# A planned attention-and-feed-forward program, replaced by one explicit list of operations

## The chip, the cores and the metric

The kernel runs on one core of one Trainium2 chip. The metric is the device time of one execution, in microseconds (us); lower is better. The core's engines run side by side and meet at semaphores: TensorE (PE in the profile, with its weight loads as PEld), VectorE (DVE), ScalarE (ACT), GpSimd (POOL) and SyncE (SP, which here only issues transfers). Each engine takes its own instructions strictly in the order in which they stand, so that an instruction that waits holds up everything behind it on that engine.

## The reference

Routed attention, and then a feed-forward layer on its output, in float32:

```python
q_assign = argmax(einsum('bhsd,hcd->bhsc', q_n, c_n))      # q_n, k_n, c_n: rows divided by their norms
k_assign = argmax(einsum('bhsd,hcd->bhsc', k_n, c_n))
mask = q_assign[:, :, :, None] == k_assign[:, :, None, :]
scores = where(mask, q @ k.T / sqrt(D), -1e9)
attn = softmax(scores)
x = (attn @ v).transpose(0, 2, 1, 3).reshape(B * S, H * D)
h = x @ w_in
out = (h * sigmoid(h)) @ w_out
```

There are B = 4 batches of H = 8 heads, S = 768 positions, D = 64, 16 clusters for each head; w_in is 512 x 2048 and w_out 2048 x 512. The output has 3072 rows of 512.

## The kernel before

**Jobs and codes.** A job holds the rows of q and k of one head of one batch (jobs 0 to 7 and two extra ones, x0 and x1, for the first batch; jobs 8 to 31 for the three others). `load` (lines 107 to 113) brings its rows in as float32, with two transfers on SP's queue. `hi` and `lo` (lines 116 to 133) split them into two halves of float16. `xpose` (line 141) is one DMA transpose, issued by SP, that turns both halves so that the 64 features lie on partitions: tile `ab<-hl`. In the first batch TensorE does this instead (`tr`, line 155, and `ev`). `logits_n` (line 180) multiplies the transposed rows with the centroids: 12 small matmuls into `psN`. `lsum`, `mx_n` and `ge_n` on VectorE turn the result into a one-hot cluster code. Up to job 15 TensorE turns the code round and SP moves it below the features (`cd_mm`, `cd_ev`); from job 16 on a DMA transpose (`c_xpose`, line 233) and a move issued by GpSimd (`c_move`, line 237) do so. A score matmul over features and code then gives a masked score in one pass.

**Score units.** There are 192 units. `qk_mm` (line 354) makes one with two matmuls of 384 columns, `exp` (line 359) takes the exponential on ScalarE. `pv` (line 371) multiplies six units of two heads with the values in 36 small matmuls, `norm` divides, and either TensorE (`xn_t`) or a DMA transpose issued by SP (`xn_d`, line 412) turns the result into a piece of `xt`. `load_v` (line 290) brings the values of one head in, and `cast_v` on GpSimd makes them float16.

**Feed-forward.** For each half batch (b, c) there are 16 hidden blocks: `unit_a` is four matmuls with w_in (line 421, tile `ph`), a tanh on ScalarE (line 441) and a gating product on VectorE (line 444, tile `gt`); below, one of them is called a hidden unit. Then come the output products with w_out, directly (`part_b`, line 480) or, for 9 pairs of blocks, by a scheme with seven products in place of eight (class `Pair`, line 562). `w_load` (lines 618 and 621) brings the weights in by 12 transfers on GpSimd's queue, numbers 0 to 7 for w_in and 8 to 11 for w_out; the last two wait for the exponentials of units 22 and 23, by a small copy of one of their elements (line 614).

**What sets the order.** Up to unit 26 the order is a list, `plan`, written out by hand. From there a planner in the kernel's own code runs through the rest: it keeps a clock for each engine with assumed lengths, a list of waiting pieces for each, and takes the piece that is ready and has the lowest rank. Due times for loads and splits stand in tables (`SPLIT`, `AHEAD`, `VALUES`, `CAST`); assumed transfer times stand in `lands`, which starts with a backlog of 13.2 us; `ROOM`, `CODES` and `TURN` are margins behind a transfer. PSUM banks 0 to 3 are handed out from a list of free ones. Values of heads 16 to 31 are loaded by GpSimd (`value_free`), those of 8 to 15 by SP.

**The end.** The last pair's last product is made in two halves of 128 columns (`product` with a part, line 562). ScalarE copies one (line 609) and VectorE the other (line 607), and each goes out by a transfer of its own (line 610).

## Time and profile before

| | |
|---|---|
| median of three runs | 302.59 us (302.19 to 305.77) |
| the profiled execution's own time | 302.92 us |
| its span, first to last instruction | 301.1 us |
| mean granted TensorE clock | 0.994 |
| PE busy | 289.7 us, 96% of the span |
| ACT, DVE, POOL busy | 223.2, 223.1, 73.2 us |
| DMA moved | 45.16 MB, mean 150 GB/s |

In the profile a span of 40 slices shows the busy share of each engine in tenths. A matmul's duration in a row (327 ns for 384 columns) is longer than its share of the engine's time, since the next one starts before it ends: in a dense stretch four of them take 0.65 us. A wait is listed by the line that waits, the line that released it, the total, how often, and the longest. A transfer's "us to landing" runs from its issue to the time when the data are there.

### The profile page before, as it was taken

To read this page: it belongs to the slowest core of one execution; us is meant where nothing else is said; L and a number is where in the kernel's file an instruction comes from. 1 tells how busy PE (TensorE), PEld (TensorE's weight loads), DVE (VectorE), ACT (ScalarE), POOL (GpSimd) and SP (SyncE) were. 2 spreads that over 40 slices of the span, in tenths; PEclk is the share of its full clock that TensorE was granted. 3 is DMA by queue.
4 is the path that set the end of the run, shared out by engine and by line. 5 is a ranking of instruction groups with operands and counts; after the bars stand their busy time and mean duration, and the time that the engine had idled before them with its cause. 6 is when DMAs were issued, how large, how long until landed. Compare 5 with 4: busy or idle time off the path is not lost.

```text
span 301.1 us, 8269 instructions
## 1 busy us (share of the span) xinstructions
PE 289.7 (96%) x3305; PEld 206.5 (69%) x3305; DVE 223.1 (74%) x467; ACT 223.2 (74%) x365; POOL 73.2 (24%) x133
## 2 busy tenths in 40 slices
PE   7889899999999999999997999999999999999995
PEld 3767756666666566678754778776777767767784
DVE  5999569587999989897764679879746375468753
ACT  5869879856997679987894897977769888455420
POOL 2884630010240037533601250522200000000000
PEclk9999999999999999999997999999999999999999
DMA  6697899996997999998699599594311003110114
GB/s 215 192 233 150 232 196 224 181 247 178 266 249 180 230 211 165 251 198 165 172 122 188 157 172 269 108 181 95 73 48 38 15 15 96 37 35 0 37 35 142
DMA packets 79574, 45.16 MB, mean 150 GB/s; under 512 B 58384, under 2 KB 75568, under 8 KB 79536
## 3 DMA queue, kind: packets, MB, share of 16 engines
q1 hardware_dynamic: 74304, 36.14, 53.3%
q0 software_dynamic: 4800, 8.13, 14.7%
q8 instruction: 26, 0.43, 0.6%
q10 hardware_dynamic: 432, 0.36, 0.4%
q14 instruction: 12, 0.10, 0.1%
HBM read 27.30 MB, written 6.29 MB: 112 GB/s over the span
## 4 chain that ended last, share of the span: by engine, by line
PE 85%; DMA 9%; DVE 2%; ACT 1%; SPq 1%; issue 0%; ACTq 0%
PE ph L421 26%; PE pS L354 18%; PE po L562 18%; PE pO L371 10%; PE po L480 7%; DMA ab<-hl 4%; PE psN L180 3%; DMA ab<-cd 2%; DMA raw<-in_k_dram 1%; DMA raw<-in_q_dram 1%; DVE hl L132 1%; ACT P L359 1%; SPq L111 1%; PE px L393 0%; PE pTk L155 0%
## 5 line engine op out<-in xcount | busy, mean ns | idle before, releaser
L359 ACT ACTIVATE P<-pS 128x768 f16<-128x768 f32 x192 | 155.9, 825 | 32.8 <-PE pS L354 32.2
L421 PE MATMUL ph<-xt,win_s 128*128 128x384 f16 x512 | 98.2, 327 | 0.2 <-DVE gt L444 0.2
L354 PE MATMUL pS<-ab 128*128 128x384 f16 x384 | 93.4, 328 | 1.6 <-DMA ab<-cd 0.8
L444 DVE SCALAR_TENSOR_TENSOR gt<-tn,ph 128x384 f16<-128x384 f32 x110 | 59.1, 549 | 30.5 <-ACT tn L441 29.9
L421 PEld LDWEIGHTS <-win_s 128*128 128x128 f16 x512 | 49.4, 98 | 31.0 <-issue 0.7
L441 ACT ACTIVATE tn<-ph 128x384 f32<-128x384 f32 x110 | 55.0, 509 | 8.3 <-PE ph L421 7.4
L354 PEld LDWEIGHTS <-ab 128*128 128x128 f16 x384 | 34.5, 98 | 18.6 <-issue 1.2
L371 PEld LDWEIGHTS <-P 128*128 128x128 f16 x1152 | 39.9, 97 | 6.0 <-DVE gt L444 1.2
L371 PE MATMUL pO<-vt,P 128*128 128x65 f16 x1152 | 41.4, 193 | 0.6 <-DVE gt L444 0.5
L562 PEld LDWEIGHTS <-gt 128*128 128x128 f16 x336 | 31.8, 98 | 6.5 <-DVE gt L544 0.4
L132 DVE SCALAR_TENSOR_TENSOR hl<-raw,hl 128x768 f16<-128x768 f32 (+3 forms) x35 | 33.0, 945 | 1.6 <-ACT hl L123 1.3
L295 POOL CAST vt<-vn 128x384 f16<-128x384 f32 x32 | 18.3, 585 | 48.6 <-DMA vn<-in_v_dram 48.6
L562 PE MATMUL po<-wout_s,gt 128*128 128x256 f16 x216 | 27.7, 273 | 0.0
L480 PE MATMUL po<-wout_s,gt 128*128 128x512 f16 x96 | 24.5, 379 | 0.0
L224 POOL TENSOR_SCALAR od<-od 128x96 f16<-128x96 f16 x16 | 9.3, 579 | 59.6 <-DVE od L217 59.5
L180 PEld LDWEIGHTS <-ab 128*128 128x128 f16 x458 | 17.1, 97 | 5.8 <-DMA ab<-hl 2.3
L180 PE MATMUL psN<-stk,ab 128*128 128x32 f16 (+1 forms) x458 | 18.4, 188 | 1.9 <-DMA ab<-hl 1.9
L192 DVE TENSOR_REDUCE L<-psN 128x192 f32<-128x384 f32 (+1 forms) x27 | 14.8, 549 | 6.2 <-PE psN L180 6.1
L562 PE MATMUL po<-tw,sg 128*128 128x256 f16 x144 | 19.0, 281 | 0.0
L383 DVE TENSOR_TENSOR xn<-pO,zr 128x384 f16<-128x384 f32 x32 | 17.8, 558 | 1.1
L562 PEld LDWEIGHTS <-sg 128*128 128x128 f16 x144 | 14.3, 100 | 3.2 <-issue 0.3
L467 ACT ACTIVATE tn<-ph 128x768 f32<-128x768 f32 x9 | 7.3, 811 | 11.4 <-PE ph L421 11.4
(101 smaller groups left out, 264.5 us busy)
## 6 DMA issues: line engine op xcount, KB each, us to landing
raw<-in_k_dram SPq DMA_DIRECT2D x31, 192.0 KB, 3.6
out_dram<-ot SPq DMA_DIRECT2D x23, 256.0 KB, 2.3
raw<-in_q_dram SPq DMA_DIRECT2D x24, 192.0 KB, 3.6
vn<-in_v_dram SPq DMA_DIRECT2D x16, 192.0 KB, 4.1
vn<-in_v_dram POOLq DMA_DIRECT2D x16, 192.0 KB, 4.5
win_s<-in_moe_w_in_dram POOLq DMA_DIRECT2D x8, 256.0 KB, 5.9
wout_s<-in_moe_w_out_dram POOLq DMA_DIRECT2D x4, 512.0 KB, 16.1
cp<-gt SPq DMA_DIRECT2D x4, 256.0 KB, 4.3
```

What stands on the lines that cost most here:

```text
L132: nc.vector.scalar_tensor_tensor(out=hl[:, s, 1, :], in0=raws[job.name][:, s, :], scalar=QS, in1=hl[:, s, 0, :], op0=ALU.mult, op1=ALU.sub ...
L180: nc.tensor.matmul(L[:, n % g, :, n // g], ab[:, i, :], stk[:, job.groups[i // 3][0], x : x + w], start=(x == 0), stop=(x + w == 2 * HC),)
L295: nc.gpsimd.tensor_copy(vt[:, :, 0:D], vns.pop(i))
L354: nc.tensor.matmul(pS[:, e, 0:HALF], abs_[kj.name][:, kn, :], rhs, start=True, stop=True)
L359: nc.scalar.activation(out=P, in_=pst.pop(u)[:, :, 0:HALF], func=AF.Exp, bias=0.0, scale=ESC)
L371: nc.tensor.matmul(o[:, (2 * t + h) * VW : (2 * t + h + 1) * VW], Ps[i + h, c, j // 2][:, j % 2, ts(t, 128)], vtb[(i + h) % 13][:, j, 0:VW ...
L383: nc.vector.tensor_tensor(out=xn, in0=ov[:, :, 0:D], in1=zr.unsqueeze(2).to_broadcast([128, 2 * NM, D]), op=ALU.mult)
L421: nc.tensor.matmul(ph[:, 0:HALF], win_s[:, r, ts(fb, 128)], xts[b, c][:, r, :], start=(r == 0), stop=(r == NR - 1))
L441: nc.scalar.activation(out=tn, in_=ph[:, 0:HALF], func=AF.Tanh, bias=0.0, scale=1.0)
L444: nc.vector.scalar_tensor_tensor(out=gt[:, fb, :], in0=tn, scalar=1.0, in1=ph[:, 0:HALF], op0=ALU.add, op1=ALU.mult)
L480: nc.tensor.matmul(po, gts[b, c][:, fc, ts(t, 128)], wout_s[:, fc, :], start=(fc == 0), stop=(fc == NFB - 1))
L562: nc.tensor.matmul(o, l[:, f, :], x[:, x0 : x0 + w], start=(f == 0 and k in begins), stop=(f == HK - 1), skip_group_check=True)
```

## The change

The planner, the hand-written plan for the first part and the list of free PSUM banks go (some 650 lines). In their place stands one string, `order`, of some 1,550 words for the whole program, and a table `words` that maps each word to a function. A word is an operation, its job, unit or block, an engine letter where there is a choice, and after @ the PSUM banks. Instructions are issued in the order of the words; each engine's own order follows from it. The computation is the same, and so are the numbers of matmuls of each kind but for one: the last product is no longer cut in two.

Some steps that one function did are now two words, so that the second can stand later: the move of the code (`cd_go`) behind its eviction, the stores of output blocks (`part_store`, `second`, `second_last`, `third_last`) behind the copies. Of the values of heads 16 to 31, twelve are now loaded by SP (S); GpSimd keeps six loads in all (P: heads 10, 15, 18, 27, 29, 30). In the first part the high halves of jobs 5 and 7 move from GpSimd to ScalarE and that of job 6 from GpSimd to VectorE.

```diff
-    def cd_mm(job):
+    def cd_mm(job, bk=None):
...
-        done(psN)
-        nc.sync.dma_start(abs_[job.name][64 : 64 + HC, 0 : 2 * m, :].rearrange("p n c -> p (n c)"), o)
+        cds[job.name] = o
+
+    def cd_go(job):
+        m = (job.n + 1) // 2
+        nc.sync.dma_start(abs_[job.name][64 : 64 + HC, 0 : 2 * m, :].rearrange("p n c -> p (n c)"), cds.pop(job.name))
...
-        def c21_last(self, part):
-            x = slice(part * HD // 2, part * HD // 2 + HD // 2)
-            if part:
-                nc.vector.tensor_copy(self.ot2[:, x], self.A[:, x])
-            else:
-                nc.scalar.activation(out=self.ot2[:, x], in_=self.A[:, x], func=AF.Copy, bias=0.0, scale=1.0)
-            (nc.sync if part else nc.scalar).dma_start(self.rows()[:, 0, x], self.ot2[:, x])
+        def c21_last(self):
+            nc.scalar.activation(out=self.ot2[:, 0:HD], in_=self.A[:, 0:HD], func=AF.Copy, bias=0.0, scale=1.0)
+
+        def third_last(self):
+            nc.scalar.dma_start(self.rows()[:, 0, :], self.ot2[:, 0:HD])
...
-        if i >= 2 * H:
-            add("POOL", t, 0.6, lambda: load_v(i, nc.gpsimd), lambda t: got_v(i, t))
-        else:
-            add("SP", t, 0.7, lambda: load_v(i), lambda t: got_v(i, t))
...
+        ab.0.0.0@2 ce.x1.A nm.6.0 s.24 cg.x1 ab.0.0.2@3 x.24 ld.10 xp.6.0@0 ab.0.0.1@1 xe.6.0.D ae.0.0.0
+        ae.0.0.1 s.25 t.0.0.0 ab.0.0.7@0 x.25 g.0.0.0 ae.0.0.7 ae.0.0.2 lo.8 ab.0.0.6@2 t.0.0.7 t.0.0.1 ae.0.0.6
+        s.26 g.0.0.7 t.0.0.6 tp.8 s.27 t.0.0.2 ab.0.0.4@0 g.0.0.6 x.26 ae.0.0.4 g.0.0.1 ab.0.0.5@2 g.0.0.2 x.27
+        ae.0.0.5 ab.0.0.3@1 t.0.0.4 s.28 ae.0.0.3 g.0.0.4 s.29 t.0.0.3 au.0.0.10@3 t.0.0.5 g.0.0.3 x.28
+        au.0.0.8@0 g.0.0.5 au.0.0.9@1 x.29 pv.0.1@2 t.0.0.8 t.0.0.9 hi.10.A g.0.0.9 s.31 s.30 nm.0.1 au.0.0.11@1
+        x.30 g.0.0.8 L.8.32@2 t.0.0.10 hi.11.D au.0.0.12@0 t.0.0.11 ls.8 x.31 s.32 g.0.0.11 au.0.0.13@2 g.0.0.10
...
+        "tp": lambda x, k: xpose(key_job(x[0])),
+        "L": lambda x, k: logits_n(key_job(x[0]), k and k[0], int(x[1]), range(int(x[2]), int(x[3])) if x[2:] else None),
+        "s": lambda x, k: qk_mm(int(x[0])),
+        "v": lambda x, k: load_v(int(x[0]), {"S": nc.sync, "P": nc.gpsimd, "A": nc.scalar}[x[1]]),
+        "w": lambda x, k: w_load(int(x[0]), int(x[1]) if x[1:] else None),
...
+    for word in order:
+        word, _, n = word.partition("@")
+        name, *rest = word.split(".")
+        words[name](tuple(rest), [int(y) for y in n] or None)
```

Three places show what moves; line numbers are those of each kernel.

The first is VectorE just after the hidden units of the first half batch begin. Before: `gt<-tn,ph` is the gate of a hidden unit, `hl<-raw` the high half and `hl<-raw,hl` the low half of a job (here jobs 8 to 11 in turn), `L<-psN` the sum of job 8's logits, made from what TensorE has just put into `psN`.

```order
L444 SCALAR_TENSOR_TENSOR gt<-tn,ph 128x384 x8
L127 TENSOR_SCALAR hl<-raw 128x12x64 x2
L132 SCALAR_TENSOR_TENSOR hl<-raw,hl 128x12x64
L444 SCALAR_TENSOR_TENSOR gt<-tn,ph 128x384
L132 SCALAR_TENSOR_TENSOR hl<-raw,hl 128x12x64
L444 SCALAR_TENSOR_TENSOR gt<-tn,ph 128x384 x2
L381 RECIPROCAL zr<-pO 128x6
L383 TENSOR_TENSOR xn<-pO,zr 128x384
```

After, from the copy of the last piece of `xt` to that sum:

```order
L393 COPY xt<-px 128x384
L432 SCALAR_TENSOR_TENSOR gt<-tn,ph 128x384
L120 SCALAR_TENSOR_TENSOR hl<-raw,hl 128x12x64
L432 SCALAR_TENSOR_TENSOR gt<-tn,ph 128x384 x8
L371 RECIPROCAL zr<-pO 128x6
L373 TENSOR_TENSOR xn<-pO,zr 128x384
L432 SCALAR_TENSOR_TENSOR gt<-tn,ph 128x384
L115 TENSOR_SCALAR hl<-raw 128x12x64
L179 TENSOR_REDUCE L<-psN 128x192
```

Job 8's low half stood behind eight gates and now stands behind one. The sum of its logits came behind 16 gates, two norms and an output copy; now it comes behind ten gates and one norm. On TensorE its 12 matmuls have moved with it, to a place before unit 32, from a place before unit 43.

The second is GpSimd with the weights. `vt` are casts of values (the number is the slot, here that of the head), `win_s` and `wout_s` the transfers of weights, `pace` the small copies that wait for an exponential. Before:

```order
L295 CAST vt_73<-vn 128x6x64
L295 CAST vt_77<-vn 128x6x64
L618 DMA win_s<-in_moe_w_in_dram 128x1024 x2
L295 CAST vt_76<-vn 128x6x64
L618 DMA win_s<-in_moe_w_in_dram 128x1024 x2
L621 DMA wout_s<-in_moe_w_out_dram 128x4x512 x2
L614 COPY pace<-P 1x1
L621 DMA wout_s<-in_moe_w_out_dram 128x4x512
```

After:

```order
L285 CAST vt_73<-vn 128x6x64
L285 CAST vt_72<-vn 128x6x64
L610 DMA win_s<-in_moe_w_in_dram 128x1024 x2
L285 CAST vt_76<-vn 128x6x64
L832 MEMSET od 128x256
L285 CAST vt_77<-vn 128x6x64
L610 DMA win_s<-in_moe_w_in_dram 128x1024 x3
L613 DMA wout_s<-in_moe_w_out_dram 128x4x512 x2
```

The slot numbers are those of the tiles (70 is head 0, so 73 is head 3). Behind head 3's cast stood four transfers of w_in and four of w_out (the eighth is behind a second pacing copy, in both); now there are five and four.

The third is GpSimd where the code moves of jobs 21 to 23 end (`ab<-cdt`). Before:

```order
L237 DMA ab<-cdt 16x6x256 x3
L295 CAST vt_81<-vn 128x6x64
L290 DMA vn<-in_v_dram 128x384 x3
L295 CAST vt_82<-vn 128x6x64
L290 DMA vn<-in_v_dram 128x384
```

After:

```order
L224 DMA ab<-cdt 16x6x256 x2
L285 CAST vt_79<-vn 128x6x64
L224 DMA ab<-cdt 16x6x256
L280 DMA vn<-in_v_dram 128x384
L211 TENSOR_SCALAR od<-od 128x2x16x3
```

Four loads of values in a row on GpSimd have become one; the others stand on SP, earlier or later. Job 24's DMA transpose, which stood beside these four loads, stands in the new list behind unit 104 (word tp.24), and its 12 logit matmuls behind unit 118 (L.24); before they stood behind units 109 and 119.

## The prediction

> **What bounds the kernel now.** I read the page first: busy times, the slices, and the chain that ended last.

> ```profile
> PE 289.7 (96%) x3305; PEld 206.5 (69%) x3305; DVE 223.1 (74%) x467; ACT 223.2 (74%) x365; POOL 73.2 (24%) x133
> PE   7889899999999999999997999999999999999995
> PEclk9999999999999999999997999999999999999999
> DMA  6697899996997999998699599594311003110114
> PE 85%; DMA 9%; DVE 2%; ACT 1%; SPq 1%; issue 0%; ACTq 0%
> ```

> TensorE is the bound: 96% busy, 85% of the chain. VectorE and ScalarE have a quarter of the span free. Since the change leaves TensorE's work as it is, the order can win or lose only what TensorE does not spend at work: the first slices (7, 8, 8), the 22nd (7, with a clock of 7), and whatever new hole it makes. The windows give their sizes; the columns are the stretch, its length, busy PE, PEld, DVE, ACT and POOL with counts, the clock, the DMA share and GB/s.

> ```profile
> 0.00:10.00 10.00, 7.92 (x82) 4.53 (x83) 6.66 (x33) 5.88 (x12) 4.33 (x14) 1.00 0.74 230
> 10.00:20.00 10.00, 8.45 (x153) 6.63 (x154) 9.58 (x23) 7.98 (x14) 8.52 (x9) 1.00 0.73 196
> 20.00:30.00 10.00, 9.17 (x155) 6.93 (x154) 9.20 (x22) 8.53 (x13) 5.72 (x7) 1.00 0.82 166
> 30.00:40.00 10.00, 9.06 (x151) 6.75 (x149) 5.08 (x15) 8.12 (x12) 7.14 (x14) 1.00 0.91 210
> 162.00:164.00 2.00, 2.00 (x10) 1.13 (x9) 1.71 (x4) 1.15 (x2) 0.54 (x2) 0.52 0.61 115
> 164.00:166.00 2.00, 2.00 (x11) 1.19 (x10) 0.00 (x0) 0.48 (x2) 0.70 (x2) 0.63 0.70 198
> ```

> In the first 40 us TensorE is idle for 40 − 34.6 = 5.4 us. From 162 to 166 it is busy but at 0.52 and 0.63 of full clock, which costs (0.48 + 0.37) × 2 = 1.7 us. TensorE's waits and the chain name what comes just before that dip:

> ```profile
> PE psN L180 <- DMA ab<-hl: 1.9, 1, 1.9
> 148.84 12.38 DMA ab<-hl
> ```

> This is job 24: its DMA transpose was issued at 148.84 and landed 12.4 us later, TensorE stood for 1.9 us, and the clock fell behind that. It is the one long wait on a transfer after the start: 1.9 + 1.7 = 3.6 us.

> **The change part by part.**

> *Job 24.* Around its transpose stand these on GpSimd and SP:

> ```profile
> 148.46 1.66 POOL L290 DMA_DIRECT2D vn<-in_v_dram  x3
> 148.84 3.66 SPq L141 DMA_TRANSPOSE ab<-hl  x1
> L141 SPq DMA_TRANSPOSE ab<-hl x14: 1464/1836/2547, 59.1 to 133.8; - x14
> DMA to landing us min/median/max: 4.0/4.8/6.0
> ```

> Three loads of values went out side by side with the transpose; fourteen transposes of quieter stretches landed in 4.0 to 6.0 us. In the new list one load is left there, and the transpose stands behind unit 104, its logits behind unit 118, 14 units apart; before, behind units 109 and 119, ten apart, which gave it 12.4 − 1.9 = 10.5 us. At the same pace 14 units give 14.7, and the 12.4 fits in without any gain from the loads. I take 1.9 and 1.7 away. What is late next are jobs with shorter leads, below.

> *The end.* The last product is cut in two no longer; its two copies, 0.29 us each one after the other, become one copy of 256 columns on ScalarE:

> ```profile
> 297.80 0.29 ACT ot L609
> 298.11 0.29 DVE ot L607
> L568 ACT ACTIVATE ot<-po x9: 384/384/453, 133.0 to 288.9; 128x256 f32<-128x256 f32 x9
> ```

> From 297.80 to 298.40 it was 0.60; now 0.38: −0.2. The eight matmuls that go are as many columns as those that take their place, so nothing more.

> *Start.* Three high halves leave GpSimd before unit 24, two for ScalarE, one for VectorE; ScalarE also takes two evictions of keys and gives up one of queries, two of codes and one of `xt`:

> ```profile
> L125 POOL TENSOR_SCALAR hl<-raw 128x576 f16<-128x576 f32 x4 | 6.6, 1652 | 4.1 <-DVE hl L132 3.2 <-PE psN L246 0.9
> L123 ACT ACTIVATE hl<-raw 128x576 f16<-128x576 f32 x3 | 2.0, 680 | 1.1 <-DMA raw<-in_q_dram 1.1
> L164 ACT ACTIVATE ab<-pTk 128x768 f16<-128x768 f16 x2 | 1.6, 800 | 0.0
> L164 ACT ACTIVATE ab<-pTq 128x384 f16<-128x384 f16 x4 | 2.0, 491 | 0.8 <-PE pTq L155 0.7
> L257 ACT ACTIVATE cd<-psN,kadd 80x256 f16<-80x256 f32 x5 | 2.3, 470 | 2.2 <-PE psN L246 2.2
> L402 ACT ACTIVATE xt<-px 128x384 f16<-128x384 f16 x3 | 1.5, 491 | 0.2 <-PE px L393 0.2
> ```

> ScalarE: 2 × 0.68 + 2 × 0.80 − 0.49 − 2 × 0.47 − 0.49 = +1.0 us, and ScalarE feeds TensorE there. Against it, each high half that TensorE may wait for comes 1.65 − 0.68 = 1.0 us earlier. No row says which ends last. I take 0; the ends are +1.5 (ScalarE's 1.0 and half a microsecond on VectorE, both in full) and −1.5 (half of the three gains of 1.0).

> *Job 8, the large term.* Its low half now stands behind the first gate on VectorE, not behind the eighth, so its DMA transpose goes out earlier, and its 12 logit matmuls stand on TensorE before unit 32, not before unit 43. When does the transpose go out?

> ```profile
> 40.49 3.32 DVE L444 SCALAR_TENSOR_TENSOR gt<-tn,ph 128x384 f16<-128x384 f32 x6 [1.14 <-ACT tn L441]
> L132 DVE SCALAR_TENSOR_TENSOR hl<-raw,hl 128x768 f16<-128x768 f32 x26 | 26.0, 999 | 1.0 <-ACT hl L123 0.7
> L141 SPq DMA_TRANSPOSE ab<-hl x2: 4200/5484/6768, 47.3 to 51.6; - x2
> DMA to landing us min/median/max: 8.8/10.3/11.8
> L621 POOL DMA_DIRECT2D wout_s<-in_moe_w_out_dram x4: 740/770/797, 35.8 to 38.3; - x4
> DMA to landing us min/median/max: 12.6/16.1/20.0
> ```

> First gate at 40.49, 3.32 / 6 = 0.55 for it, 1.0 for the low half: 42.0, against 47.3 before. That is in the midst of the second weights, of which the last was issued at 38.3 and took 20.0 us, to 58.3. Before, jobs 8 and 9 were transposed in the same crowd: 47.3 + 11.8 = 59.1 and 51.6 + 8.8 = 60.4. When does TensorE get to job 8's logits? In the new order 32 units (64 matmuls), 12 hidden units (48) and five blocks of `pO` (180) stand before them. Before, just that much had begun by 49.6:

> ```profile
> L354 PE MATMUL pS<-ab x64: 322/326/337, 11.7 to 47.7; 128*128 128x384 f16 x64
> L421 PE MATMUL ph<-xt,win_s x48: 323/326/326, 37.9 to 49.5; 128*128 128x384 f16 x48
> L371 PE MATMUL pO<-vt,P x180: 191/193/203, 24.5 to 48.9; 128*128 128x65 f16 x180
> ```

> So TensorE is there at about 49.8, and the lead is 49.8 − 42.0 = 7.8 us. The landing lies between a quiet 5 us (47.0, no wait) and the end that job 9 had (60.4, a wait of 10.6). I take the row nearest in kind, the same transpose in the same crowd, 11.8: landing at 53.8, a wait of 4.0 us. A dip follows, as behind the one wait of this kind: 1.7. Nothing covers it, since TensorE works in its order; behind the logits are queued unit 32 and all after it, and ScalarE's exponentials run dry. [...]

> *Late values on SP.* Of the values of heads 16 to 31 twelve are loaded by SP; each occupies its queue for about half a microsecond and stands in front of transposes. SP waits for nothing on TensorE's path there, so I cost it at nothing; its cover is the lead of each transpose, and the shortest gives a rival.

> The sum, against the profiled execution's own 302.92 us (span 301.1): −1.9 − 1.7 − 0.2 + 0 + 4.0 + 1.7 = 304.8. That execution is 0.3 above the median of the three runs, 302.59; so 304.5.

> **The rivals.**

> *No wait at job 8.* If the transpose lands by 49.8, within 7.8 us, only the gains are left: 302.92 − 3.8 = 299.1, as a median 298.8, and with the ends of the start 297.3 to 300.3. For it: a transpose takes 4.0 to 6.0 us in quiet stretches, and in before two transposes shared the crowd. Against it: none issued while weights were landing took less than 8.8.

> *Slower: job 8 lands with the end of the weights.* If the crowd gives the transpose no more than what is left until the weights are in, issuing it early brings nothing: it lands where job 9's did, 60.4, the wait is 10.6, and the time 302.92 − 3.8 + 10.6 + 1.7 = 311.4, as a median 311.1. For it: both transposes ended within 2.1 us behind the last weights, 58.3, whatever their issue, and the fifth transfer of w_in stands closer to them. Against it: of jobs 8 and 9 each would then have been starved in full, and the DMA share there was not all taken by weights. It is slower by over 2% from a landing at about 58.

> *Loads on SP in a transpose's way.* Job 25 has a short lead in the new list: five units, two `po` blocks, one `pO` block and one hidden unit.

> ```profile
> 131.87 0.87 PE po L562 x8
> 48.04 1.09 PE pO L371 x36
> 49.13 0.65 PE ph L421 x4
> L141 SPq DMA_TRANSPOSE ab<-hl x2: 3659/4516/5373, 148.8 to 155.1; - x2
> DMA to landing us min/median/max: 8.7/10.5/12.4
> ```

> At half of four matmuls' 0.65 for each unit, 5 × 0.33 + 2 × 0.87 + 1.09 + 0.65 = 5.1 us, with waits some 5.9. If it lands in 8.7, as before, TensorE waits 2.8 and the clock dips for 1.7: alone 299.1 + 4.5 = 303.6, as a median 303.3. For it: the loads now go out from the queue that the transposes use. Against it: fewer of them together. [...]

> **How the numbers follow.** The wait at job 8: 0.53, at 304.5; its own range is from a landing at 51.8 (a wait of 2, 302.5) to one at 57.5 (7.7, 308.2). No wait: 0.30. Landing with the weights: 0.12. A wait at job 25 and none at job 8: 0.05. The range takes in the no-wait case with its start's best end, 297.3, and the main case to its end with a little of a second wait, 309.0; left out are the slower rival and a start that gains more, some 0.17. A measurement of this kernel can tell about 2% from no change: 296.5 and 308.6. Faster than that needs the no-wait case and 2.3 us more from the start, of 5.4 idle: 0.07. Slower: the 0.12 and the last of the main case, 0.14. Within: 0.79.

> **What would show it.** Right: in the list of TensorE's waits the longest is that of `psN` on `ab<-hl`, once, of 2 to 8 us, near 50 us, with a dip of the clock behind it; job 8's transpose is issued near 42 and takes over 8 us; no wait near 160, and the 22nd slice has 9 for both busy share and clock. The no-wait case: the transpose lands before 49.8, all slices from the fifth on are 9. The slower rival: a slice of 0 to 3 near 55. Job 25's: a wait past 150 again. The forecast is wrong altogether if TensorE's idle time in the first 40 us leaves 5.4 by more than 1.5 either way, or if a wait stands where none of these names one.

## The result, and the profile after

The changed kernel takes 317.14 us (median of 6 runs, 315.82 to 320.20) against 301.27 us before (median of 6 runs, 298.96 to 305.77): 1.0553 times as long, 95% interval 1.0483 to 1.0623. A ratio counts no run over 1.5% above the fastest of its kernel (here it leaves out the one of 305.77), so it is not the quotient of the two medians. The forecast was 304.5 us, with a range of 297.3 to 309.0; what came is the rival that ended slower, and more. The execution that was profiled took 315.82 us, the shortest of the six, with a span of 314.0.

The page of the changed kernel, the rows that answer to those shown of before:

```profile
PE 292.4 (93%) x3297; PEld 207.4 (66%) x3297; DVE 217.9 (69%) x462; ACT 227.1 (72%) x372; POOL 60.5 (19%) x120
PE   7897993599997999899999999999999999999996
PEclk9999999699999799999999999999999999999999
DMA  7788999268979778989987957796352102110012
PE 68%; DMA 16%; DVE 5%; SPq 4%; POOL 3%; issue 2%; ACT 1%; DVEq 0%; ACTq 0%
```

The busy time of TensorE is almost what it was; the span has grown around it. Two holes are new: slices 7 and 8 (3 and 5 in tenths busy, a clock of 6 in the 8th) and slice 13 (7, with a clock of 7 in the 14th). The old one, the 22nd slice, is closed. On the chain the DMA has 16% where it had 9%. TensorE's waits name the holes, and the chain gives the transfers behind them:

```profile
PE psN L167 <- DMA ab<-hl: 10.7, 2, 8.6
PE pO L361 <- POOL vt L285: 1.5, 1, 1.5
PE junk L622 <- DVE zz L632: 1.2, 1, 1.2
PE ph L409 <- DVE L L179: 1.2, 1, 1.2
...
41.86 16.21 DMA ab<-hl
58.12 0.82 PE psN L167 x12
93.41 8.41 DMA ab<-hl
101.86 0.75 PE psN L167 x12
```

The first, 8.6 us, is job 8: its DMA transpose went out at 41.86 and landed 16.2 us later, at 58.1, while TensorE had stood since 49.5. The second, 10.7 − 8.6 = 2.1 us, is job 14, of which the forecast said nothing. The 1.5 us on `vt` lie in the start. The third of the new ones is 1.2 us near 125: the sum of job 17's logits stood on VectorE behind a high half whose raw rows had not come, as the timeline of VectorE shows:

```profile
126.05 0.56 DVE L115 TENSOR_SCALAR hl<-raw 128x768 f16<-128x768 f32 x1 [2.10 <-DMA raw<-in_k_dram]
126.53 0.55 DVE L179 TENSOR_REDUCE L<-psN 128x192 f32<-128x384 f32 x1
```

In the first of these waits and behind the second the clock fell (from 54 to 56, while TensorE still stood at job 8, it was 0.55 already). The windows show what it was when TensorE worked again (columns as before: the clock is the third number from the end):

```profile
58.00:60.00 2.00, 1.88 (x16) 1.22 (x17) 1.02 (x3) 0.00 (x0) 0.50 (x1) 0.50 0.00 0
60.00:62.00 2.00, 2.00 (x11) 1.09 (x10) 0.86 (x2) 1.10 (x3) 0.00 (x0) 0.74 0.00 0
102.00:104.00 2.00, 2.00 (x16) 1.01 (x15) 1.35 (x3) 0.00 (x0) 0.68 (x2) 0.50 1.07 336
104.00:106.00 2.00, 2.00 (x9) 1.01 (x8) 0.90 (x3) 0.89 (x2) 0.51 (x1) 0.65 1.30 173
```

That is 1.88 × 0.50 + 2 × 0.26 = 1.5 us behind job 8 and 2 × 0.50 + 2 × 0.35 = 1.7 behind job 14. Together: 302.92 − 3.6 (the old wait and dip) − 0.2 (the end) + 8.6 + 1.5 + 2.1 + 1.7 + 1.2 = 314.2. Of the other 1.6 us to 315.82, waits of half a microsecond and less after 150 give 0.8 (1.3 in all, where before has 0.5); the rest is not traced to a place.

### The profile page after: what moved, and what is told of

It is laid out like the page before. It is cut to its first block, busy times and chain, and to the rows that moved or that the text cites. A ratio compares the mean times of both kernels' runs of the same rounds, so it can differ in the third digit from the quotient of the medians.

```text
span 314.0 us, 8190 instructions
## 1 busy us (share of the span) xinstructions
PE 292.4 (93%) x3297; PEld 207.4 (66%) x3297; DVE 217.9 (69%) x462; ACT 227.1 (72%) x372; POOL 60.5 (19%) x120
## 4 chain that ended last, share of the span: by engine, by line
PE 68%; DMA 16%; DVE 5%; SPq 4%; POOL 3%; issue 2%; ACT 1%; DVEq 0%; ACTq 0%
PE ph L409 23%; PE po L554 14%; PE pS L344 14%; DMA ab<-hl 11%; PE pO L361 8%; PE po L467 5%; DMA raw<-in_k_dram 3%; PE psN L167 2%; SPq L99 2%; DVE hl L120 2%; POOL hl L113 1%; DMA raw<-in_q_dram 1%; POOL vt L285 1%; DMA xt<-xn 1%; SPq L220 1%
## 5 line engine op out<-in xcount | busy, mean ns | idle before, releaser
L349 ACT ACTIVATE P<-pS 128x768 f16<-128x768 f32 x192 | 149.7, 813 | 41.1 <-PE pS L344 39.9
L409 PE MATMUL ph<-xt,win_s 128*128 128x384 f16 x512 | 97.0, 328 | 2.1 <-DVE L L179 1.2
L344 PE MATMUL pS<-ab 128*128 128x384 f16 x384 | 88.4, 328 | 0.3
L432 DVE SCALAR_TENSOR_TENSOR gt<-tn,ph 128x384 f16<-128x384 f32 x110 | 57.9, 549 | 26.7 <-ACT tn L429 26.1
L409 PEld LDWEIGHTS <-win_s 128*128 128x128 f16 x512 | 49.6, 99 | 33.7 <-issue 4.0
L429 ACT ACTIVATE tn<-ph 128x384 f32<-128x384 f32 x110 | 50.6, 497 | 12.9 <-PE ph L409 11.4
L554 PEld LDWEIGHTS <-gt 128*128 128x128 f16 x328 | 31.7, 98 | 6.5 <-DVE gt L535 0.2
L120 DVE SCALAR_TENSOR_TENSOR hl<-raw,hl 128x768 f16<-128x768 f32 (+3 forms) x35 | 31.1, 897 | 1.6 <-ACT hl L111 1.3
L167 PE MATMUL psN<-stk,ab 128*128 128x32 f16 (+1 forms) x458 | 18.9, 190 | 11.2 <-DMA ab<-hl 10.7
L211 POOL TENSOR_SCALAR od<-od 128x96 f16<-128x96 f16 x16 | 10.0, 623 | 72.2 <-DVE od L204 72.1
L554 PE MATMUL po<-tw,sg 128*128 128x256 f16 x144 | 17.7, 273 | 0.0
L467 PEld LDWEIGHTS <-gt 128*128 128x128 f16 x96 | 9.2, 100 | 8.8 <-issue 0.6
```

What stands on the lines that cost most here:

```text
L120: nc.vector.scalar_tensor_tensor(out=hl[:, s, 1, :], in0=raws[job.name][:, s, :], scalar=QS, in1=hl[:, s, 0, :], op0=ALU.mult, op1=ALU.sub ...
L167: nc.tensor.matmul(L[:, n % g, :, n // g], ab[:, i, :], stk[:, job.groups[i // 3][0], x : x + w], start=(x == 0), stop=(x + w == 2 * HC),)
L344: nc.tensor.matmul(pS[:, e, 0:HALF], abs_[kj.name][:, kn, :], rhs, start=True, stop=True)
L349: nc.scalar.activation(out=P, in_=pst.pop(u)[:, :, 0:HALF], func=AF.Exp, bias=0.0, scale=ESC)
L409: nc.tensor.matmul(ph[:, 0:HALF], win_s[:, r, ts(fb, 128)], xts[b, c][:, r, :], start=(r == 0), stop=(r == NR - 1))
L429: nc.scalar.activation(out=tn, in_=ph[:, 0:HALF], func=AF.Tanh, bias=0.0, scale=1.0)
```

## The experiments

The lines of the diffs are words of the list; "..." stands for words left out.

### Job 8: did TensorE only ask too soon?

```diff
- ... x.30 g.0.0.8 L.8.32@2 t.0.0.10 ...
+ ... x.30 g.0.0.8 t.0.0.10 ...
- ... xe.2.1.A x.40 s.41 ld.12 b.0.0.0.3 xe.0.1.A x.41 v.9.S ...
+ ... xe.2.1.A x.40 s.41 L.8.32@2 ld.12 b.0.0.0.3 xe.0.1.A x.41 ls.8 mx.8 ge.8 v.9.S ...
```

> The changed kernel with job 8's 12 logit matmuls and what VectorE makes of them moved from before unit 32 to behind unit 41; nothing else. Theory 1 (job 8's transpose lands only when the last weights are in, near 58, and TensorE merely asked too soon): TensorE now gets there at about 61, the wait of 8.6 us and the dip behind it, 1.5 us, are gone, jobs 9 to 11 go out earlier, and the time falls from 317.1 by about 10 us to 307. Rival (the loss only moves: TensorE then waits for the last piece of w_out or for the transposes of jobs 9 to 11 in the same crowd): a new wait of 3 us or more between 50 and 70, time 310 or more.

Measured: 309.64 us (4 runs, 308.60 to 311.06), 1.0307 times before (1.0245 to 1.0370). The transpose itself did as badly as ever (41.89, landed at 58.0), but TensorE got to it at 60.45 and the hole is gone:

```profile
PE   6898999999969998999899999999999999999995
PEclk9999999999997999999799999999999999999999
...
PE psN L167 <- DMA ab<-hl: 4.4, 2, 2.4
PE pS L344 <- DMA ab<-cd: 1.4, 2, 0.9
PE junk L622 <- DVE zz L632: 1.2, 1, 1.2
PE ph L409 <- DVE L L179: 0.8, 1, 0.8
```

So this one place costs 317.14 − 309.64 = 7.5 us, somewhat less than half of the loss. It was to be 10: behind it a wait came up that the changed kernel did not have, 2.0 us at job 23, beside the 2.4 us at job 14, each with a dip of 1.7 us.

### Job 8: why 16 us?

Three runs change what is in flight when the transpose goes out, and leave the logits where the change put them. The first holds back the transpose, the others the weights:

```diff
- ... ae.0.0.2 lo.8 ab.0.0.6@2 ... t.0.0.6 tp.8 s.27 ...
+ ... au.0.0.8@0 g.0.0.5 lo.8 tp.8 au.0.0.9@1 ...
```

> The changed kernel with job 8's low half and transpose behind eight gates on VectorE, as before the change (issue at 46 to 47 in place of 41.9); its logits stay before unit 32. Theory 1 (the landing follows the end of the weights, whatever the issue): it still lands at 57.5 to 59.5, 11 to 13 us after its issue, and the time is that of the changed kernel within 1.5 us. Rival (the transpose gets a constant share in the crowd and needs some 16 us there): it lands at 61 to 63 and the time grows by 3 to 5 us. Rival (it needs some 12 us, and 16.2 was an accident): landing as in theory 1, but then the last weights, not the transpose, end elsewhere.

```diff
- ... w.10.22 xe.2.0.D ... xe.4.0.D w.11.23 hi.8.D ...
+ ... x.30 w.10.30 g.0.0.8 ... x.32 w.11.32 s.33 ...
```

> The changed kernel with the third and fourth transfer of w_out (512 KB each) held until the exponentials of units 30 and 32, some 12 us later than now; job 8 untouched. Theory 1 (the weights in flight hold up job 8's transpose): with half of w_out out of its way the transpose, issued near 42, lands by 46 to 50, the wait falls from 8.6 to under 1.5 us and the time by 7 to 10 us, unless TensorE then waits for the late pieces of w_out. Rival (the transpose is slow for its own sake, or behind the loads of raw rows in SP's own queue): it lands near 58 still and the wait stays at 8 us or more.

```diff
- ... s.22 w.8 xe.0.0.D pv.4.0.1.x w.9 x.22 ... w.10.22 xe.2.0.D ... w.11.23 hi.8.D ...
+ ... x.27 w.8.27 ... x.28 w.9.28 ... x.30 w.10.30 ... x.32 w.11.32 ...
```

> The changed kernel with all four transfers of w_out held until the exponentials of units 27, 28, 30 and 32, so that none is in flight when job 8's transpose goes out near 42; its logits stay before unit 32. With half of them held it landed at 52.7, 1 us behind the two that were left. Theory (it lands when the weights in flight are in): it now lands by 46 to 49.5, 4 to 7 us after its issue, no wait at job 8 over 0.5 us; then TensorE may wait for the late first piece of w_out near 55. Rival (the raw rows of jobs 9 and 10 and the last of w_in hold it as much): it lands after 50, a wait of 1 us or more.

The transpose of job 8 in the changed kernel and in these three, in that order, each from the answer on its line in a window around its issue:

```profile
L129 SPq DMA_TRANSPOSE ab<-hl x1: 4485/4485/4485, 41.9 to 41.9; - x1
DMA to landing us min/median/max: 16.2/16.2/16.2
```

```profile
L129 SPq DMA_TRANSPOSE ab<-hl x1: 4562/4562/4562, 47.1 to 47.1; - x1
DMA to landing us min/median/max: 10.1/10.1/10.1
```

```profile
L129 SPq DMA_TRANSPOSE ab<-hl x1: 4559/4559/4559, 42.2 to 42.2; - x1
DMA to landing us min/median/max: 10.5/10.5/10.5
```

```profile
L129 SPq DMA_TRANSPOSE ab<-hl x1: 1893/1893/1893, 42.0 to 42.0; - x1
DMA to landing us min/median/max: 4.3/4.3/4.3
```

Issued 5.2 us later it landed 0.9 us earlier (57.1). With half of the weights held back it landed at 52.7, with all of them held back at 46.3, in 4.3 us. The weights in flight are the cause: it landed 0.3, 1.5 and 1.1 us behind the last of those in the first three kernels (57.8, 55.6 and 51.6), whenever it was issued. The raw rows in SP's own queue, the other suspect, were there in the last run too, and it took 4.3 us. The times of these single runs: 319.91, 312.62 and 310.61 us. The first is 2.8 us over the median of the changed kernel, not within 1.5 as expected, with a wait of 2.4 us near 158 that the changed kernel does not have; the second gained 4.5 us, not 7 to 10. With all held back there was no wait at job 8; with half of them there was one of 2.9 us, not the 0 to 1.5 that was expected.

What the DMA engines did in that time can be counted from the packet records of the traces. Packets begun in each microsecond, q0 being GpSimd's queue (the weights, 1 KB a packet), q1 SP's (256 B a packet for the transpose, which has 12 × 128 = 1536 of them; up to 45 also raw rows of jobs, 1.5 KB a packet); each time is from the start of its own span:

```
 us    changed kernel    transpose late    all w_out late
         q0    q1          q0    q1          q0    q1
 44     114   116         113   114           0   527
 45     164    64         165    68           0   640
 47     160   155         206     0         179     0
 49     156   153         202     0
 51     156   154         167    86
 54     154   157          59   505
 55     145   174          16   252
 56      72   158           0   446
```

While both queues had packets, from 47 to 52, the changed kernel's began in nearly equal numbers, 153 to 161 a microsecond on each queue. At 156 a microsecond 1536 packets need 9.8 us, and the queue with the small packets had a fifth of the bytes (39 of 198 KB in the microsecond from 49). With no weights beside it, all 1536 packets of the same transpose began within 2.5 us (43.3 to 45.8), some 610 a microsecond. In the run with the transpose late, it was issued at 47.07 and its first packet began at 50.98: 3.9 us went by first, with no raw rows ahead of it. So the 16.2 us of the changed kernel are 4.2 us until the first packet, 11.1 us (46.0 to 57.1) beside the packets of the weights, with a hole in the 53rd microsecond (34 and 42 packets), and 1.0 us from the last packet to the landing. With these sizes it ended close to the last weights; in the run with the transpose late, 505 of its packets began in the microsecond from 54, beside 59 on GpSimd's queue.

### Job 14: raw rows ahead, or loads of values behind?

> The changed kernel with job 14's transpose moved on SP to just behind job 13's, ahead of the four loads of raw rows of jobs 15 and 16 and of a code move; nothing else. Theory (the second loss, 2.1 us of wait and a clock of 0.50 and 0.65 for 4 us behind it, 1.7 us, is a lead too short for a transpose that shares the DMA engines with those loads): it goes out about 3 us earlier, lands before 97, the wait near 100 and the dip go, and the time falls by 3 to 4 us. Rival (the loads of values issued behind it slow it as much wherever it stands): it still takes 8 us, TensorE waits for less than 1 us all the same, but the dip stays.

```diff
- ... ld.15 ls.12 ... ld.16 ge.12 ... cg.12 au.0.1.6@1 nm.8.0 tp.14 L.13.32@3 ...
+ ... tp.13 tp.14 t.0.1.2 s.52 ... ld.15 ls.12 ... ld.16 ge.12 ... cg.12 au.0.1.6@1 nm.8.0 L.13.32@3 ...
```

Measured: 323.66 us, 6.5 us slower, in a single run. The wait at job 14 did go (its transpose landed at most 5.6 us after its issue, though the same loads followed it), but TensorE waited 2.5 us at nearly the same time for a gate, and the clock fell behind that:

```profile
PE psN L167 <- DMA ab<-hl: 12.8, 3, 8.8
PE ph L409 <- DVE gt L432: 3.3, 3, 2.5
...
98.85 0.56 DVE L115 TENSOR_SCALAR hl<-raw 128x768 f16<-128x768 f32 x1 [2.79 <-DMA raw<-in_k_dram]
99.33 1.48 DVE L432 SCALAR_TENSOR_TENSOR gt<-tn,ph 128x384 f16<-128x384 f32 x3
```

The loads of raw rows now stood behind two transposes on SP. Job 15's rows came late, its high half waited on VectorE for 2.8 us, and the gates stood behind it. Among the rest of the 6.5 us are waits of 1.9 and 2.2 us at two other transposes, near 159 and 188.

Two runs ask the same of the list with job 8 mended. In one only job 16's two loads go behind the transpose; in the other the twelve late loads of values are GpSimd's again:

```diff
- ... mx.12 t.0.1.4 ld.16 ge.12 ... nm.8.0 tp.14 L.13.32@3 ...
+ ... mx.12 t.0.1.4 ge.12 ... nm.8.0 tp.14 ld.16 L.13.32@3 ...
```

> The list with job 8's logits behind unit 41 (309.6 us), and in it the two loads of raw rows of job 16 moved on SP from ahead of job 14's transpose to just behind it; nothing else. Theory (what is issued ahead of the transpose holds it up, the four loads of raw rows within 3 us; what is issued behind it hardly does): it goes out about 1 us earlier and lands within 6 to 7 us, the wait of 2.4 us near 92 falls under 0.7 and its dip of 1.7 us goes, and the time falls by 2.5 to 4 us. Rival (the loads behind it count as much as those ahead): it lands after 8 to 9 us as now, TensorE waits for 1 to 2 us still.

```diff
- v.16.S v.17.S v.19.S v.20.S v.22.S v.21.S v.24.S v.23.S v.25.S v.26.S v.28.S v.31.S
+ v.16.P v.17.P v.19.P v.20.P v.22.P v.21.P v.24.P v.23.P v.25.P v.26.P v.28.P v.31.P
```

> The list with job 8's logits behind unit 41 (the first experiment, 309.6 us), and in it the twelve loads of values of heads 16 to 31 that the change gave to SP are issued by GpSimd again, at the same places of the list; nothing else. Theory (it does not matter which engine issues them; the DMA engines are shared): job 14's transpose still lands after 8 to 9 us, the waits near 92 and 147 stay at 2.0 to 2.4 us, and the time is 309.6 within 1.5 us. Rival (the loads of values in SP's queue are what the transposes wait behind): job 14's transpose lands within 6 us, at least one of the two waits goes, and the time falls by 3 us or more. Rival on the other side: GpSimd's casts of values come later behind its issues, a new wait of the product with values, and the time grows by 2 us or more.

Job 14's transpose with job 8 mended, then with job 16's loads behind it, then with the values by GpSimd, and for the last the loads on GpSimd beside it:

```profile
L129 SPq DMA_TRANSPOSE ab<-hl x1: 2089/2089/2089, 83.1 to 83.1; - x1
DMA to landing us min/median/max: 8.8/8.8/8.8
```

```profile
L129 SPq DMA_TRANSPOSE ab<-hl x1: 2683/2683/2683, 83.6 to 83.6; - x1
DMA to landing us min/median/max: 6.1/6.1/6.1
```

```profile
L129 SPq DMA_TRANSPOSE ab<-hl x1: 2273/2273/2273, 84.0 to 84.0; - x1
DMA to landing us min/median/max: 11.2/11.2/11.2
...
84.43 1.70 POOL L280 DMA_DIRECT2D vn<-in_v_dram  x3
```

What stood ahead of the transpose in its own queue counted: two of four loads less, 2.7 us less, no wait at job 14 (306.61 us, a single run; 2.5 to 4 us less were expected, 3.0 came). And the landing changed with the edit, against the theory: on SP two of these loads went out 3.6 us behind the transpose and the third by GpSimd; issued by GpSimd, all three went out in a burst 0.5 us behind it, in the other queue, and it took 11.2 us and TensorE waited 4.8. The edit changes queue and moment together, so the run does not say which of them counts. Nor did the packets begin in nearly equal numbers here, as beside the weights: in the microsecond from 88, 5 packets began on GpSimd's queue (up to 4.6 KB each) and 108 of 256 B on SP's. How these few could hold up the transpose is not shown. The time, 309.35 us (2 runs), hardly moved: in the profiled execution the wait of 2.0 us at job 23 and its dip were not there.

### One part of the change in the kernel before

```diff
-        if i >= 2 * H:
+        if i >= 2 * H and i < 26:
             add("POOL", t, 0.6, lambda: load_v(i, nc.gpsimd), lambda t: got_v(i, t))
```

> The kernel before with one part of the change alone: the loads of values of heads 26 to 31 are given to SP in place of GpSimd, and its planner places them; so no burst of three stands beside job 24's transpose. Theory (the 12.4 us landing there came from that burst): job 24's transpose lands within 7 us, the wait of 1.9 us and the dip of 1.7 us go, and the time falls by 1 to 3.5 us from that of the kernel before. Rival (on SP they stand in the way of other transposes): a wait of 1 us or more on another job between 150 and 200, time within 1 us of before or above it.

Job 24's transpose in that kernel, with the loads of values on SP behind it:

```profile
149.81 2.91 SPq L141 DMA_TRANSPOSE ab<-hl  x1
152.77 1.05 SPq L290 DMA_DIRECT2D vn<-in_v_dram  x2
...
DMA to landing us min/median/max: 5.7/5.7/5.7
```

5.7 us, where it took 12.4 beside three loads by GpSimd; the wait and the dip are gone, and its profiled execution has the shortest span of all that were profiled, 299.5 us. And yet its time, a median of 302.27 us (10 runs), is 1.0078 times that of before (1.0034 to 1.0122). The landing came out as the theory said, the gain did not. The planner places everything behind that point anew, so the run does not say what took it. A part of the answer may be that there was less to gain: before's own runs beside it have a median of 300.08 us, where the profiled one took 302.92, and the twelve of them that the ratio counts have a mean granted clock of 0.998 to 1.000, where the profiled one's is 0.994. A dip of 1.7 us lowers the mean clock by 0.006 over 301 us. So these twelve do not have the dip that the forecast took away.

### Mending what the traces name

Three leads at once on top of job 8: job 16's loads as above, job 23's logits later, job 20's high half behind the sum that it held up. Then three more.

```diff
- ... pc.1.0.p L.23.32@1 xd.14.1 ...
+ ... x.103 s.104 L.23.32@1 nm.16.0 ...
- ... x.75 tp.18 L.17.32@2 hi.20.D xp.14.0@1 ...
+ ... ls.17 xe.14.0.D s.77 lo.19 hi.20.D s.78 ...
```

> Three tight places of the list mended at once, on top of job 8's logits behind unit 41 (309.6 us): job 16's loads behind job 14's transpose, job 23's logits from behind unit 99 to behind unit 104, and the high half of job 20, which waits for its raw rows on VectorE, from ahead of the sum of job 17's logits to behind job 19's low half. Theory (the rest of the loss is a sum of such leads, 2.4 + 1.7 near 92, 2.0 + 1.7 near 147, 0.8 near 117): the time falls by 6 to 8.5 us to 301 to 303.5, about the kernel before. Rival (each wait that goes only lays bare the next one, because every lead in the list is short): new waits of together 3 us or more, and 305 or more.

```diff
- ... s.64 L.15.32@1 x.64 ld.19 b.0.1.0.2 ls.15 ...
+ ... s.64 x.64 ld.19 b.0.1.0.2 L.15.32@1 ls.15 ...
- ... nm.14.1 L.22.32@0 x.98 s.99 v.23.S ... cx.20 ... L.23.32@1 xd.14.1 x.100 ...
+ ... nm.14.1 xd.14.1 L.22.32@0 x.98 s.99 v.23.S ... cx.20 ...
- ... ld.28 au.1.1.8@1 ... v.28.S ... ld.26 ... ld.27 ... ls.24 tp.25 s.119 ...
+ ... ld.28 tp.25 au.1.1.8@1 ... v.28.S ... ld.26 ... ld.27 ... ls.24 s.119 ...
```

> The list with four leads mended (median 304.65, its profiled execution 302.56), and three more: job 15's logits one block of the product later, head 14's second transpose of outputs ahead of a load and a code move on SP, job 25's transpose ahead of two loads and a code load. Theory (the loss is a sum of short leads): the waits of 0.4, 1.0 and 0.7 us near 97, 146 and 169 go, the profiled execution takes 300.5 to 301 and the median falls by 1.5 to 3 us, to the kernel before within 1%. Rival (each mended lead shortens another): a new wait of 0.7 us or more, median 304 or more.

Measured: 304.65 us (4 runs, 302.56 to 309.24; the three that the ratio counts have a median of 303.51), 1.0107 times before (1.0025 to 1.0190); and with three more 304.34 us (4 runs, 303.02 to 305.36), 1.0108 (1.0046 to 1.0170). The first gained 6.1 us by the three runs, the lower end of the 6 to 8.5 expected, and 5.0 by all four. The second gained nothing, as its rival said: the waits it was after went, and others came:

```profile
PE pO L361 <- POOL vt L285: 1.9, 2, 1.5
PE pS L344 <- DMA ab<-cdt: 1.5, 1, 1.5
PE junk L622 <- DVE zz L632: 1.2, 1, 1.2
PE pS L344 <- ACT P L349: 1.1, 1, 1.1
```

A code move is now late by 1.5 us and an exponential by 1.1. By the ratios the mended leads gave back 4.5 of the 5.5 per cent that the change cost; the last per cent is not traced to a place, and no version here beats the kernel before.

## Why the prediction was wrong

**What bounds the kernel, the start and the end** were read rightly. TensorE's idle time in the first 40 us is 5.3 us (5.4 before), the last copy takes 0.38 us, the wait and the dip at job 24 went. The zero at the start is a balance and in part luck: a wait of 1.5 us on a cast of values came, and two of 0.8 at score units and 0.8 on transposed keys went. Job 8's transpose went out at 41.9 (42.0 forecast), and TensorE got to its logits at 49.5 (49.8).

**The step that failed is the landing of job 8's transpose**: "I take the row nearest in kind, the same transpose in the same crowd, 11.8". It took 16.2, and the wait was 8.6 us instead of 4.0. The row was of the same kind but of another time. Before, the transpose was issued 11 us before the weights ended: 104 to 160 of its packets a microsecond from 51 to 56, and then 404 and 342 as the weights thinned out. Issued 5.4 us earlier it had some 156 a microsecond and no quiet end. In this crowd the landing was a rate and a number of packets, not a duration that could be carried along with the instruction. Of the 11.0 us between the sum, 304.8, and the profiled 315.82, this step is 4.4 (4.6 of wait, and 0.2 less of dip); the leads of the next paragraph but one are 5.0, and 1.6 is the rest named with the result.

**The slower rival had the mechanism nearly right and too low a chance.** It said that the transpose lands with the weights, and gave 311.1 us with a landing at 60.4; it landed at 58.1. What I held against it ("jobs 8 and 9 each would then have been starved in full") does not follow: job 8's transpose was not starved but had about one packet in two (153 of 309 in the microsecond from 49), and with its small packets it landed 0.3 us behind the last weights all the same.

**Not among the cases: the other short leads.** I looked for jobs that could be late by what is issued between transpose and logits in the list, found job 25, and priced it. It was read 0.2 us after its landing, without a wait. The second loss was job 14 (2.1 + 1.7 us) and the third job 20's raw rows on VectorE (1.2). The reason is in the margins: from landing to reading, before, one of the jobs 8 to 31 was late, two had 1.1 us or less and sixteen over 2; after, two were late, seven had 1.1 us or less and eleven over 2. I took one lead at a time with quiet durations, and counted no loads of raw rows ahead of a transpose in its own queue. That four of them stand ahead of job 14's was there to be read in the new order (they went out from 90.5 to 92.2, the transpose at 93.4).

**Late values on SP, costed at nothing.** No run shows a cost of them. On SP they went out behind the transpose, on GpSimd beside it, and the transpose landed sooner with them on SP: 8.8 us with SP against 11.2 with GpSimd at job 14, 5.7 against 12.4 at job 24, in one execution each.

**The dips.** I gave each wait of this kind 1.7 us. Both waits of the changed kernel had one, 1.5 and 1.7. But the gain of 1.7 at job 24 was taken from one execution, and twelve others, named above, do not have that dip. Nor does the length of a wait sort them: behind job 14's 2.1 us the clock fell, behind the 2.9 us in the run with half of the weights held back it did not. What sorts them in these traces stands in the last section.

## What to carry to other kernels

Beside the weights, 1536 packets of 256 B took 11.1 us from the first to the last, where they took 2.5 us with no weights in flight. Count the packets of such a transfer, read from a trace at what pace they begin in that crowd (here some 156 a microsecond), and do not carry a duration from a row where the crowd was about to end. When a list of instructions is rewritten, make a table of the margin between landing and reading for every transfer that TensorE waits for, before looking at any one of them: thin margins at nine places told more here than the price of any one. In these runs, bulk loads that were not urgent cost an urgent small transfer least behind it in its own queue (6.1 and 5.7 us to landing), more ahead of it there (8.8), and most beside it in another (11.2 and 12.4); each is one execution.

## What the runs showed of the hardware

While weights were in flight in the changed kernel, nearly as many packets began on one queue as on the other, 156 and 153 in a microsecond, though they were of 1 KB and 256 B; with no weights beside them the small ones began at some 610 a microsecond. With the loads of values by GpSimd the numbers were not alike (5 on its queue and 108 on SP's in one microsecond). A DMA transpose showed no packet for 3.9 to 4.2 us after its issue while weights were in flight (job 8's in eleven traces), and for 1.3 us where none were.

The clock did not fall behind every wait of 2 to 3 us. In the run with half of the weights held back TensorE waited 2.9 us at 52.8 and 1.9 at 95.3, and the clock stayed at full speed; behind 1.8 us at 176.9 it fell:

```profile
54.00:56.00 2.00, 2.00 (x14) 1.21 (x13) 1.70 (x5) 1.70 (x4) 0.49 (x2) 1.00 0.91 150
96.00:98.00 2.00, 2.00 (x14) 1.11 (x12) 1.97 (x5) 0.97 (x2) 0.11 (x1) 1.00 1.08 326
178.00:180.00 2.00, 1.63 (x6) 0.77 (x6) 2.00 (x4) 0.64 (x1) 1.20 (x3) 0.53 0.12 18
```

| kernel | step, us | TensorE busy in it | clock in the next step |
|---|---|---|---|
| half of the weights held back | 48.40 to 51.81 | 1.42 us (0.42) | 1.00 |
| | 92.77 to 96.18 | 1.55 us (0.46) | 1.00 |
| | 174.69 to 178.10 | 1.33 us (0.39) | 0.50 |
| changed kernel | 98.57 to 101.98 | 1.32 us (0.39) | 0.50 |
| before | 158.66 to 162.07 | 1.50 us (0.44) | 0.50 |

The end of each left out, the twelve traces have 14 steps at full clock with half clock behind them, and TensorE was busy for 0.44 or less of each. Of all others at full clock only the first two of the table were busy for less than half. So in these twelve traces the dips went with the idle time in one step, not with the length of a wait: the wait of 2.9 us ended at 52.8 and was shared by two steps, the one of 1.8 us fell into one. What the chip itself goes by is not shown; no run varied it. Half clock for one step of 3.41 us is 1.7 us of work, about the size of the dips above (1.5 to 1.7). The border is not sharp as the traces give it (0.42 without a dip, 0.44 with one). The first record came at 4.0 to 7.2 us of the span, at another time in each trace. Whether that is why one execution of a kernel has a dip and the next has none, no run here tests.
